# Moving two weight blocks ahead of the second half of the first x array, and four float32 second stages in place of six

## The chip, the cores and the metric

The kernel runs on one core of a Trainium2 chip. The metric is the device time of one execution in microseconds, as the median of several runs. Engines are named as in the profile: PE does matrix products (PEld is its weight load), DVE is the vector engine, ACT the scalar engine, POOL the GpSimd engine, and SP issues most of the DMA transfers. All inputs lie in HBM as the reference's types, so the two weight matrices and x are read in the layouts the host prepared, and the kernel does all the arithmetic.

## What is computed

The input x has 4 batches of 3008 rows of 256 numbers. A two-dimensional Fourier transform is taken of each batch and only its real part is kept; each of the 12032 rows then goes through a two-layer network with a SiLU between the layers.

```python
def _attn_ref(x):
    X = np.fft.fft(x, axis=1)
    X = np.fft.fft(X, axis=2)
    return X.real.astype(np.float32)

def _moe_ref(x, w_in, w_out):          # w_in 256 x 2048, w_out 2048 x 256
    h = x @ w_in
    g = h * (1.0 / (1.0 + np.exp(-h)))
    return (g @ w_out).astype(np.float32)
```

## The kernel before

The transform along the 256 columns is folded into w_in: `project(q)` multiplies a block of 256 of the 2048 columns of w_in with a cosine and sine table on PE, so there are eight blocks, q = 0 to 7. The transform along the rows is done by folding x (sums and differences on DVE and POOL) and multiplying the folded rows with cosine tables on PE. The result is cut into classes of columns that are laid one behind the other in chunks; the first chunk, c = 0, has 376 columns.

For each chunk c there are 16 steps f, one for each 128 of the 2048 hidden units. A step has these parts:

- `first(c, f)`: six matmuls on PE into a PSUM tile `pq`. There are two such tiles, so the first product of step n waits until DVE has read that of step n-2.
- `act(c, f)`: three DVE instructions (L420, L421, L422) make `h` from `pq`, then ACT applies SiLU. In chunk 0, for f < `FULL`, the result stays float32 (`g`, L427). Otherwise ACT writes SiLU (L433) and a rounded high part `gh` (L434), and DVE makes the rest `gl = h - gh` (`rest`, L446).
- `second(c, f)`: it runs three steps later (`LAG = 3`). With a float32 `g` it is one float32 matmul for each of four outputs (L461); otherwise it is three matmuls in the rounded type for each output (L463, L464, L470).

Step numbers n count from chunk 0, so in chunk 0 n = f. The weights arrive as 8-byte numbers. `load_w(q)` loads a block of w_in into a `win` tile (four of them), `upper(q)` on ACT (L78) and `lower(q)` on DVE (L82) put the float32 together, `convert(q)` is both, `project(q)` is its matmul (L533), `large(q)` on ACT (L538, L540) takes the high part `abh` out of PSUM, and `small(q)` on DVE (L544) makes the low part `abl`. `load_wo(q)`, `upper_wo`, `lower_wo` do the same for the eight blocks of w_out. A block of w_out with q < FULL/2 is kept in float32 (`wo_f32`) and split later by `split_wo` (L124 on ACT, L126 on DVE); the others are split at once by `high_wo` on ACT (L116) and `low_wo` on POOL (L119).

Before step 0 the start has to deliver the folded x rows of the first class. They come in three parts: `x2_first` (`first_x2`), and the two halves h = 0 and 1 of x1 (`load_first(h)`, one transfer of 512 KB called `raw` and two of 256 KB called `minus`; `first_x1` adds them up on DVE, L199 to L208). `product(a, i)` multiplies each part with its table (L597), `spread_first` moves the result from PSUM to the tile `uv` (ACT L394, DVE L396) and writes its first row `row0` (ACT L398). In step 0 `first_row` broadcasts this row with a matmul (L670) and an ACT copy (L671) into `ub`, which the first L420 needs.

The order of instructions is written out by hand and each engine runs its own in that order. The loads on SP's queue use eight semaphores in turn, so that each waits until the one eight places ahead of it has landed, and for its tile to be free. Between the steps two queues of deferred work are drained: one of DVE and ACT pieces that build the operand of the next class and run `split_wo`, and one of POOL pieces.

Of the kernel before, what the change touches and what calls it, by code (L numbers as in the profile page):

```python
# [42 lines left out]
STARTS = [sum(CHUNKS[:j]) for j in range(len(CHUNKS))]  # L43
LAST = len(CHUNKS) - 1
LAG = 3
FULL = 6
NF = DFF // 128


# [1 line left out]
def fft_mlp(ctx, tc, x1, x2, x2_first, w_in, w_out, te, to, t2, t2f, rot1, rot2, dft, out):  # L51
# [21 lines left out]
    def load_raw(t, block):  # L73
        nc.sync.dma_start(out=t[:, 1:1 + 8 * D].rearrange("p (c n) -> p c n", c=2), in_=block)  # L74

    def upper(dst, raw):
        flat = dst.rearrange("p c n -> p (c n)")
        nc.scalar.activation(flat.bitcast(F16)[:, 1::2], raw.bitcast(BF16)[:, 4:4 + 8 * D:4], AF.Copy)  # L78

    def lower(dst, raw):  # L80
        t = dst.rearrange("p c n -> p (c n)").bitcast(U32)
        stt(t, raw.bitcast(U32)[:, 1:1 + 4 * D:2], 13, t, op0=ALU.logical_shift_right, op1=ALU.bitwise_or)  # L82

    wo = [[wts.tile([128, 2, D], F32R, name=f"woh{f}") for f in range(NF // 2)], {}]
    wo_f32 = [wts.tile([128, 2, D], F32, tag="wof", name="wof", bufs=FULL // 2 + 1) for _ in range(FULL // 2)]
    for q in range(FULL // 2, NF // 2):
        wo[1][q] = wts.tile([128, 2, D], F32R, name=f"wol{q}")
# [6 lines left out]
    def load_wo(q):  # L94
        if 3 <= q < 6:
            t = wr.tile([128, RAW], U16, tag="win", name="wo", bufs=4)
        else:
            tag = {0: "ri0", 1: "xh", 2: "xl", 6: "ri0", 7: "ri1"}[q]
            t = (xs if tag[0] == "x" else fold_p).tile([128, RAW], U16, tag=tag, name="wo")
        wo_raw[q] = t  # L100
        load_raw(t, w_out[q * 256:(q + 1) * 256, :].bitcast(U16).rearrange("(f p) d -> p f d", p=128))
# [5 lines left out]
    def upper_wo(q):  # L107
        if q < FULL // 2:
            wo_wide[q] = wo_f32[q]
        upper(wo_wide[q], wo_raw[q])  # L110
# [10 lines left out]
    def split_wo(q):  # L121
        wf, wh = wo_f32[q], wo[0][q]
        wl = wo[1][q] = wts.tile([128, 2, D], F32R, tag="wof", name="wol", bufs=FULL // 2 + 1)
        nc.scalar.activation(wh, wf, AF.Copy)  # L124
# [265 lines left out]
    def spread_first(po):  # L390
        uvh, uvl, ub, n, _ = chunk(0)
        for i in range(2):
            p = po[i][:, 0, :n]
            nc.scalar.activation(uvh[:, i, :n], p, AF.Copy)  # L394
            yield
            tt(uvl[:, i, :n], p, uvh[:, i, :n].bitcast(F32), op=ALU.subtract)  # L396
            yield
        nc.scalar.activation(row0, p[0:1], AF.Copy)  # L398
        yield
# [3 lines left out]
    def first(c, f):  # L403
        uvh, uvl, _, n, _ = chunks[c]
        fs = slice(f * 128, (f + 1) * 128)
        pq = pqs[c, f] = pq_tile()
        for i in range(2):
            po = pq[:, i, :n]
            nc.tensor.matmul(po, abh[:, i, fs], uvh[:, i, :n], start=True, stop=False)  # L409
            nc.tensor.matmul(po, abh[:, i, fs], uvl[:, i, :n], start=False, stop=False)  # L410
            nc.tensor.matmul(po, abl[:, i, fs], uvh[:, i, :n], start=False, stop=True)  # L411
# [4 lines left out]
    def act(c, f, fill=()):  # L416
# [6 lines left out]
        for fn, q in fill:  # L423
            fn(q)
        if c == 0 and f < FULL:
            g = gp.tile([128, 2, CH], F32, tag=("gh", "gl")[f % 2], name="g")
# [12 lines left out]
    def rest(c, f):  # L439
        if c == 0 and f < FULL or (c, f) in rested:  # L440
            return
        rested.add((c, f))
        gh, gl, g = gs[c, f]
        n = chunks[c][3]
        for sg in signs(c, f):
            tt(gl[:, sg, :n], g[:, sg, :n], gh[:, sg, :n].bitcast(F32), op=ALU.subtract)  # L446
# [67 lines left out]
    win, wf32, pws = {}, {}, {}  # L514

    def load_w(q):
        win[q] = wr.tile([128, RAW], U16, tag="win", name="win", bufs=4)
        load_raw(win[q], w_in[:, q * 256:(q + 1) * 256].bitcast(U16).rearrange("(c p) f -> p c f", p=128))

    def clear(q):  # L520
        wf32[q] = fold_p.tile([128, 2, 256], F32, tag="half", name="wf", bufs=3)
        nc.gpsimd.memset(wf32[q], 0.0)

    def convert(q):
        upper(wf32[q], win[q])
        lower(wf32[q], win.pop(q))

    def project(q):
        w = wf32.pop(q)
        pw = pws[q] = ps.tile([128, 2, 256], F32, tag="ps", name="pw")  # L530
        for m in range(2):
            for c in range(2):
                nc.tensor.matmul(pw[:, m, :256], dft_sb[:, c, m, :], w[:, c], start=c == 0, stop=c == 1)  # L533

    def large(q):
        fs = slice(q * 256, (q + 1) * 256)
        row = rows[32 * (q % 4):32 * (q % 4) + 1, q // 4]
        nc.scalar.activation(row, pws[q][0:1, 1, :256].rearrange("o (f p) -> o p f", p=128), AF.Copy)  # L538
        nc.gpsimd.dma_start(out=a128[q], in_=row)
        nc.scalar.activation(abh[:, :, fs], pws[q][:, :, :256], AF.Copy)  # L540

    def small(q):
        fs = slice(q * 256, (q + 1) * 256)
        tt(abl[:, :, fs], pws.pop(q)[:, :, :256], abh[:, :, fs].bitcast(F32), op=ALU.subtract)  # L544
        for a in (abh, abl):
            nc.gpsimd.memset(a[0:1, 1, fs].bitcast(F32), 0.0)
# [10 lines left out]
    def load_first(h):  # L557
        t = raw_x[0, 0, h] = raws.tile([128, 4, D], F32, tag="raw", name="raw")
        nc.sync.dma_start(out=t, in_=x1[0, :, 0, h])
        for j in range(2):  # L560
            t = minus[h, j] = gp.tile([128, 2, D], F32, tag=("gh", "gl")[j], name="minus", bufs=LAG)
            nc.sync.dma_start(out=t, in_=x1[0, :, 1, h, 2 * j:2 * j + 2])
# [33 lines left out]
    def product(a, i):  # L596
        nc.tensor.matmul(po[i][:, 0, :CLASS[0][1]], x3[:, a, 128 * i:128 * i + 128], t2f_sb[:, a],  # L597
                         start=a == 2, stop=a == 1 - i)
# [1 line left out]
    convert(0)  # L600
    project(0)
    load_w(4)
    load_first(1)
    convert(1)
    project(1)
    clear(3)
    convert(2)
    large(0)
    project(2)
    clear(4)  # L610
    small(0)
    convert(3)
    load_w(5)
    load_w(6)
    load_w(7)
    for q in range(3):
        load_wo(q)
# [17 lines left out]
    lower(wf32[4], win.pop(4))  # L635
    load_wo(3)
    project(4)
    next(x1_work[1])
    large(3)
    next(x1_work[1])  # L640
    product(1, 0)
    product(1, 1)
    product(0, 1)
    upper(wf32[5], win[5])
    upper(wf32[6], win[6])
    small(1)
    lower(wf32[5], win.pop(5))
    load_wo(4)
    project(5)
    first_spread = spread_first(po)  # L650
    next(first_spread)
    next(first_spread)
    small(2)
    next(first_spread)
    next(first_spread)
    next(first_spread)
    lower(wf32[6], win.pop(6))
    load_wo(5)
    clear(7)
    small(3)  # L660
    large(4)
    upper(wf32[7], win[7])
    small(4)
    lower(wf32[7], win.pop(7))


    def first_row():
        n = CLASS[0][1]
        p = ps.tile([128, 512], F32, tag="ps", name="ub")[:, :n]
        nc.tensor.matmul(p, ones, row0, start=True, stop=True)  # L670
        nc.scalar.activation(chunk(0)[2][:, :n], p, AF.Copy)  # L671
# [63 lines left out]
    for n in range(len(steps) + LAG):  # L735
        c, f = steps[min(n, len(steps) - 1)]
        if n < len(steps):
            first(c, f)
        if n == 0:
            first_row()  # L740
            large(5)
        if n < 2:
            project(6 + n)
            large(6 + n)
        if n >= LAG:
            second(*steps[n - LAG])
        new = None
        if n < len(steps):
            turn = turns.get((c, f)) if n < len(steps) else None
            if turn:  # L750
                drain(queue, upto=("op", turn))
                drain(pool_queue, upto=("x", turn))
                new = pq_tile()
                transform(turn, new)
            act(c, f, fills.get(n, ()))
        if n == 0:
            small(5)
        if n == 1:
            small(6)
            small(7)  # L760
        for fn, q in after.get(n, ()):
            fn(q)
        if n == 2:
            late.close()
            acc_p = ctx.enter_context(tc.tile_pool(name="acc", bufs=1, space=PSUM))
            load_wo(7)
        if 1 <= n <= len(steps):
            rest(*steps[n - 1])
        if new:
            rest(c, f)  # L770
            spread(turn, new)
        if n < len(steps):
            for fn, a in plan.get((c, f), ()):
                fn(*a)
            drain(queue, 0.6)

            if f != 1 or c == 0 or pool_queue and pool_queue[0][0][0] == "x":
                drain(pool_queue, 1.3)
# [106 lines left out]
```

## Time and profile before

| what | us |
|---|---|
| median of 3 runs | 877.68 (877.65 to 877.82) |
| the profiled execution, whole time | 877.21 |
| its span on the core | 875.4 |
| PE busy in the span | 866.1 |
| DVE busy in the span | 706.2 |
| ACT busy in the span | 508.9 |
| POOL busy in the span | 197.9 |

The profile is of one execution, which was 0.47 us below the median. Starts are counted from the start of the span. Busy times of PE are modelled from pipelined matmuls; an engine's time shown as idle is followed by what released it. Consecutive instructions of one engine overlap a little, so the distance from one start to the next can be shorter than the duration in the row.

### The profile page before, as it was taken

What the parts mean: (1) busy time and instruction counts of PE and PEld (TensorE: products, weight loads), DVE (VectorE), ACT (ScalarE), POOL (GpSimd) and SP (SyncE); (2) the same over time, 40 slices, a digit from 0 to 9 for tenths busy, and PEclk for the clock granted to TensorE, in tenths of its full rate; (3) what the DMA queues carried; (4) which work ended last, traced back from release to release, by engine and by line L of the source; (5) the groups of instructions that cost most, each with busy time, mean ns of one, the idle gap of its engine ahead of it and who ended that gap; (6) DMA issues with size and microseconds to landing.
All of it is one profiled execution on the core that took longest, in us unless ns stands there. A gap on an engine that the chain in (4) does not pass through costs nothing.

```text
span 875.4 us, 11058 instructions
## 1 busy us (share of the span) xinstructions
PE 866.1 (99%) x4138; PEld 750.2 (86%) x4138; DVE 706.2 (81%) x994; ACT 508.9 (58%) x646; POOL 197.9 (23%) x243
## 2 busy tenths in 40 slices
PE   7999999999999999999999999999999999999998
PEld 6789999999998888888888888888888888888886
DVE  5999888888897887879778877888877877777774
ACT  4677756565765564557566455557546555455554
POOL 3475541312522220243312310050300110000000
PEclk9999999999999999999999999999999999999999
DMA  9955342236231433224225201323011021200101
GB/s 333 313 177 84 106 53 53 37 58 93 10 106 26 76 77 58 44 11 112 34 30 124 9 1 50 56 48 57 1 8 49 0 10 48 10 0 5 44 1 47
DMA packets 23413, 53.81 MB, mean 61 GB/s; under 512 B 3648, under 2 KB 12224, under 8 KB 22976
## 3 DMA queue, kind: packets, MB, share of 16 engines
q1 hardware_dynamic: 19632, 38.62, 20.4%
q0 software_dynamic: 3728, 14.49, 8.6%
q8 instruction: 32, 0.52, 0.3%
q14 instruction: 21, 0.17, 0.1%
HBM read 37.86 MB, written 12.34 MB: 57 GB/s over the span
## 4 chain that ended last, share of the span: by engine, by line
PE 97%; DMA 1%; DVE 1%; SPq 1%; issue 0%; ACT 0%; DVEq 0%
PE acc L470 20%; PE acc L464 20%; PE acc L463 20%; PE pq L409 10%; PE pq L410 10%; PE pq L411 10%; PE pq L340 5%; PE acc L461 2%; DMA minus<-in_x_dram 1%; PE pw L533 1%; PE pq L597 0%; SPq L74 0%; SPq L569 0%; DVE sm L204 0%; DVE sm L200 0%
## 5 line engine op out<-in xcount | busy, mean ns | idle before, releaser
L433 ACT ACTIVATE h<-h 128x1004 f32<-128x1004 f32 (+3 forms) x204 | 199.3, 977 | 303.6 <-DVE h L422 300.4
L463 PE MATMUL acc<-gh,woh 128*128 128x502 f32 (+2 forms) x808 | 302.2, 374 | 0.0
L464 PE MATMUL acc<-gh,wol 128*128 128x502 f32 (+2 forms) x808 | 302.2, 374 | 0.0
L446 DVE TENSOR_TENSOR gl<-h,gh 128x1004 fp32r<-128x1004 f32 (+3 forms) x204 | 237.9, 1167 | 14.7 <-ACT gh L434 14.0
L420 DVE SCALAR_TENSOR_TENSOR h<-ub,a,pq 128x502 f32<-128x502 f32 (+2 forms) x208 | 144.8, 696 | 96.7 <-PE pq L411 92.5
L470 PE MATMUL acc<-gl,woh 128*128 128x502 f32 (+2 forms) x808 | 210.3, 374 | 0.0
L434 ACT ACTIVATE gh<-h 128x1004 fp32r<-128x1004 f32 (+3 forms) x204 | 199.4, 977 | 6.5
L464 PEld LDWEIGHTS acc<-gh,wol 128*128 128x128 f32 x808 | 152.4, 189 | 22.4
L463 PEld LDWEIGHTS acc<-gh,woh 128*128 128x128 f32 x808 | 152.0, 188 | 22.3
L470 PEld LDWEIGHTS acc<-gl,woh 128*128 128x128 f32 x808 | 149.6, 188 | 23.2
L409 PE MATMUL pq<-uv,abh 128*128 128x502 f32 (+2 forms) x416 | 157.7, 379 | 0.0
L410 PE MATMUL pq<-uv,abh 128*128 128x502 f32 (+2 forms) x416 | 154.8, 372 | 0.0
L411 PE MATMUL pq<-uv,abl 128*128 128x502 f32 (+2 forms) x416 | 154.6, 372 | 0.0
L421 DVE TENSOR_TENSOR h<-h,pq 128x502 f32<-128x502 f32 (+2 forms) x208 | 132.7, 638 | 7.2
L422 DVE TENSOR_TENSOR h<-h,pq 128x502 f32<-128x502 f32 (+2 forms) x208 | 132.6, 638 | 7.2
L322 POOL TENSOR_TENSOR xl<-xf,xh 128x256 fp32r<-128x256 f32 x53 | 53.0, 1027 | 365.4 <-ACT xh L315 306.1
L409 PEld LDWEIGHTS pq<-uv,abh 128*128 128x128 f32 x416 | 78.1, 188 | 12.3 <-DVE h L422 0.5
L410 PEld LDWEIGHTS pq<-uv,abh 128*128 128x128 f32 x416 | 78.2, 188 | 11.7
L411 PEld LDWEIGHTS pq<-uv,abl 128*128 128x128 f32 x416 | 78.1, 188 | 11.4
L234 POOL TENSOR_TENSOR ri<-ri,raw 128x256 f32<-128x256 f32 x24 | 23.1, 978 | 57.6 <-ACT ri L229 57.3
L478 ACT ACTIVATE o<-acc 128x502 f32<-128x502 f32 (+2 forms) x52 | 27.9, 559 | 9.8 <-PE acc L470 7.7
L387 DVE TENSOR_TENSOR uv<-pq,uv 128x752 fp32r<-128x752 f32 (+4 forms) x21 | 14.5, 716 | 21.2 <-ACT row L383 21.1
(113 smaller groups left out, 472.5 us busy)
## 6 DMA issues: line engine op xcount, KB each, us to landing
raw<-in_x_dram SPq DMA_DIRECT2D x22, 512.0 KB, 6.3
raw<-in_x_dram POOLq DMA_DIRECT2D x20, 512.0 KB, 7.5
out_dram<-o SPq DMA_DIRECT2D x36, 251.0 KB, 2.2
win<-in_w_in_dram SPq DMA_DIRECT2D x8, 512.0 KB, 8.1
wo<-in_w_out_dram SPq DMA_DIRECT2D x8, 512.0 KB, 8.0
out_dram<-o SPq DMA_DIRECT2D x12, 188.0 KB, 2.3
ub<-row SPq DMA_DIRECT2D x8, 188.0 KB, 8.6
te<-in_te_dram POOLq DMA_DIRECT2D x1, 1128.0 KB, 5.5
```

The source lines that it names most:

```text
L409: nc.tensor.matmul(po, abh[:, i, fs], uvh[:, i, :n], start=True, stop=False)
L410: nc.tensor.matmul(po, abh[:, i, fs], uvl[:, i, :n], start=False, stop=False)
L411: nc.tensor.matmul(po, abl[:, i, fs], uvh[:, i, :n], start=False, stop=True)
L420: stt(p[:, :n], ub[:, :n], a128[f // 2][:, f % 2:f % 2 + 1], pq[:, 0, :n], op0=ALU.mult, op1=ALU.add)
L421: tt(h[:, 0, :n], p[:, :n], pq[:, 1, :n], op=ALU.add)
L422: tt(h[:, 1, :n], p[:, :n], pq[:, 1, :n], op=ALU.subtract)
L433: nc.scalar.activation(h[:, sg, :n], h[:, sg, :n], AF.Silu)
L434: nc.scalar.activation(gh[:, sg, :n], h[:, sg, :n], AF.Copy)
L446: tt(gl[:, sg, :n], g[:, sg, :n], gh[:, sg, :n].bitcast(F32), op=ALU.subtract)
L463: nc.tensor.matmul(po, wo[0][f // 2][:, f % 2, es], gh[:, sg, :n], start=f == 0, stop=False)
L464: nc.tensor.matmul(po, wo[1][f // 2][:, f % 2, es], gh[:, sg, :n], start=False, stop=False)
L470: nc.tensor.matmul(accs[c][i][:, :n], wo[0][f // 2][:, f % 2, es], gl[:, sg, :n], start=False, stop=f == NF - 1)
```

## The change

`FULL` goes from 6 to 4: steps 4 and 5 of chunk 0 and block 2 of w_out go the way of the later ones. In the start, the loads of w_in blocks 5 and 6 stand ahead of `load_first(1)` in SP's queue, and their conversion and projection stand ahead of `first_x1` of the second half. `small(1)` and `small(2)` move with them. Block 7 is converted before step 0 as it was, but projected within step 0, ahead of the first product of step 1, and not in step 1. `large` and `small` follow their blocks. Nothing is taken away from the start: all eight blocks are still loaded, converted and projected once.

```diff
--- before.py
+++ after.py
@@ -43,7 +43,7 @@
 STARTS = [sum(CHUNKS[:j]) for j in range(len(CHUNKS))]
 LAST = len(CHUNKS) - 1
 LAG = 3
-FULL = 6
+FULL = 4
 NF = DFF // 128
 
 
@@ -600,18 +600,18 @@
     convert(0)
     project(0)
     load_w(4)
-    load_first(1)
     convert(1)
     project(1)
+    load_w(5)
     clear(3)
     convert(2)
     large(0)
     project(2)
+    load_w(6)
+    load_first(1)
     clear(4)
     small(0)
     convert(3)
-    load_w(5)
-    load_w(6)
     load_w(7)
     for q in range(3):
         load_wo(q)
@@ -635,33 +635,34 @@
     lower(wf32[4], win.pop(4))
     load_wo(3)
     project(4)
+    small(1)
+    large(3)
+    convert(5)
+    load_wo(4)
+    project(5)
+    clear(7)
+    small(2)
+    convert(6)
+    load_wo(5)
+    project(6)
+    large(4)
     next(x1_work[1])
-    large(3)
+    large(5)
     next(x1_work[1])
     product(1, 0)
     product(1, 1)
     product(0, 1)
-    upper(wf32[5], win[5])
-    upper(wf32[6], win[6])
-    small(1)
-    lower(wf32[5], win.pop(5))
-    load_wo(4)
-    project(5)
+    small(3)
     first_spread = spread_first(po)
     next(first_spread)
     next(first_spread)
-    small(2)
+    small(4)
     next(first_spread)
     next(first_spread)
     next(first_spread)
-    lower(wf32[6], win.pop(6))
-    load_wo(5)
-    clear(7)
-    small(3)
-    large(4)
-    upper(wf32[7], win[7])
-    small(4)
-    lower(wf32[7], win.pop(7))
+    convert(7)
+    large(6)
+    small(5)
 
 
     def first_row():
@@ -738,10 +739,9 @@
             first(c, f)
         if n == 0:
             first_row()
-            large(5)
-        if n < 2:
-            project(6 + n)
-            large(6 + n)
+            project(7)
+        if n == 1:
+            large(7)
         if n >= LAG:
             second(*steps[n - LAG])
         new = None
@@ -754,9 +754,8 @@
                 transform(turn, new)
             act(c, f, fills.get(n, ()))
         if n == 0:
-            small(5)
+            small(6)
         if n == 1:
-            small(6)
             small(7)
         for fn, q in after.get(n, ()):
             fn(q)
```

Three places show how the instructions moved. The first is DVE around the second half of x1. L82 is `lower`, L544 is `small`, and L200 and L202 belong to `first_x1` of that half. This is one piece of the difference, with + for the changed kernel.

```order
 L208 TENSOR_TENSOR xf<-xf 128x127
 L82 SCALAR_TENSOR_TENSOR wf<-win,wf 128x512
+L544 TENSOR_TENSOR abl<-pw,abh 128x2x256
+L82 SCALAR_TENSOR_TENSOR wf<-win,wf 128x512
+L544 TENSOR_TENSOR abl<-pw,abh 128x2x256
+L82 SCALAR_TENSOR_TENSOR wf<-win,wf 128x512
 L200 TENSOR_TENSOR sm<-raw 128x512
 L202 TENSOR_TENSOR sm<-sm,minus 128x512
```

`small(1)`, `lower(5)`, `small(2)` and `lower(6)` now stand between `lower(4)` and the second half of x1; before, they followed it.

The second place is ACT from the two copies of the spread (L394) to the copy of the broadcast row into `ub` (L671, which is L672 in the changed kernel). Before:

```order
L394 ACTIVATE uv<-pq 128x376 x2
L398 ACTIVATE once<-pq 1x376
L538 ACTIVATE once<-pw 1x256
L540 ACTIVATE abh<-pw 128x2x256
L78 ACTIVATE wf<-win 128x512
L671 ACTIVATE ub<-ub 128x376
```

And in the changed kernel:

```order
L394 ACTIVATE uv<-pq 128x376 x2
L398 ACTIVATE once<-pq 1x376
L78 ACTIVATE wf<-win 128x512
L538 ACTIVATE once<-pw 1x256
L540 ACTIVATE abh<-pw 128x2x256
L672 ACTIVATE ub<-ub 128x376
```

The conversion of block 7 (L78) now stands ahead of a `large` (L538, L540, now that of block 6), and both still stand ahead of `ub`.

The third place is DVE in steps 5 and 6, where L82 is `lower_wo` and L300 to L301 are pieces of the next operand.

```order
 L422 TENSOR_TENSOR h<-h,pq 128x376
 L82 SCALAR_TENSOR_TENSOR wf<-wo,wf 128x512
+L446 TENSOR_TENSOR gl<-h,gh 128x2x376
 L300 TENSOR_TENSOR xf<-sm 64x129
 L301 TENSOR_TENSOR xf<-sm 64x127
```

An L446 is added there, and a second one in the same way a step later; they are the `gl` of steps 4 and 5.

## Rows read from the trace of the kernel before

**Rows 1.** The page: busy times of the engines; a costly group (busy, mean ns, idle).

```profile
PE 866.1 (99%) x4138; PEld 750.2 (86%) x4138; DVE 706.2 (81%) x994; ACT 508.9 (58%) x646; POOL 197.9 (23%) x243
...
L434 ACT ACTIVATE gh<-h 128x1004 fp32r<-128x1004 f32 (+3 forms) x204 | 199.4, 977 | 6.5
```

**Rows 2.** Busy time of each engine by stretch, then granted clock, DMA share, GB/s.

```profile
37.00:42.00 5.00, 5.00 (x21) 3.35 (x20) 4.90 (x11) 2.56 (x4) 3.36 (x8) 1.00 0.95 229
...
57.00:62.00 5.00, 5.00 (x30) 5.00 (x30) 4.83 (x6) 2.15 (x3) 5.00 (x6) 1.00 0.93 371
...
200.00:400.00 200.00, 199.99 (x973) 175.28 (x973) 165.56 (x236) 116.19 (x149) 50.47 (x57) 1.00 0.34 58
```

**Rows 3.** Waits of PE from 23 us to the end: us in total, times, longest.

```profile
PE pq L597 <- DVE xf L207: 0.9, 1, 0.9
```

**Rows 4.** Timeline of PE's weight load at step 13.

```profile
72.40 0.19 PEld L409 LDWEIGHTS pq<-uv,abh 128*128 128x128 f32 x1 [0.31 <-DVE uv L387]
```

**Rows 5.** Timeline of DVE in the start and step 0.

```profile
20.09 0.68 DVE L82 SCALAR_TENSOR_TENSOR wf<-win,wf 128x512 uint32<-128x512 uint32 x1
20.69 0.69 DVE L200 TENSOR_TENSOR sm<-raw 128x512 f32<-128x512 f32 x1
...
26.69 0.54 DVE L396 TENSOR_TENSOR uv<-pq,uv 128x376 fp32r<-128x376 f32 x1
...
30.02 0.60 DVE L420 SCALAR_TENSOR_TENSOR h<-ub,a,pq 128x376 f32<-128x376 f32 x1
...
31.70 0.68 DVE L544 TENSOR_TENSOR abl<-pw,abh 128x512 fp32r<-128x512 f32 x1
```

**Rows 6.** Timeline of ACT in the start.

```profile
19.09 0.78 ACT L78 ACTIVATE wf<-win 128x512 f16<-128x512 bf16 x1 [1.44 <-DMA win<-in_w_in_dram]
...
20.34 0.60 ACT L540 ACTIVATE abh<-pw 128x512 fp32r<-128x512 f32 x1
...
24.48 0.78 ACT L78 ACTIVATE wf<-win 128x512 f16<-128x512 bf16 x1 [0.29 <-DMA win<-in_w_in_dram]
...
25.93 0.48 ACT L394 ACTIVATE uv<-pq 128x376 fp32r<-128x376 f32 x1 [0.33 <-PE pq L597]
27.26 0.47 ACT L398 ACTIVATE once<-pq 1x376 f32<-1x376 f32 x1 [0.85 <-DVE uv L396]
...
...
30.01 0.37 ACT L538 ACTIVATE once<-pw 1x256 f32<-1x256 f32 x1
```

**Rows 7.** Timeline of SP's queue: issues of the third w_out block and of `rot_sb`.

```profile
20.28 0.37 SPq L74 DMA_DIRECT2D wo<-in_w_out_dram  x1
...
21.63 0.34 SPq L619 DMA_DIRECT2D rot_sb<-in_rot_dram  x1
```

**Rows 8.** The chain that ended last, in order of time: start, us, what.

```profile
23.75 2.13 PE pq L597 x6
...
28.64 0.82 PE ub L670 x2
...
32.42 1.73 PE pw L533 x8
...
36.19 2.69 PE acc L461 x8
...
39.91 2.53 PE acc L461 x8
...
57.67 0.17 PE acc L463
```

**Rows 9.** Timeline of DVE in steps 6 to 12.

```profile
53.16 0.94 DVE L446 TENSOR_TENSOR gl<-h,gh 128x752 fp32r<-128x752 f32 x1
...
57.79 1.48 DVE L446 TENSOR_TENSOR gl<-h,gh 128x752 fp32r<-128x752 f32 x1
...
71.40 0.95 DVE L387 TENSOR_TENSOR uv<-pq,uv 128x756 fp32r<-128x756 f32 x1
```

**Rows 10.** Timeline of POOL beside DVE's steps 7 and 8.

```profile
56.04 1.28 POOL L119 TENSOR_TENSOR wol<-wf,woh 128x512 fp32r<-128x512 f32 x1
```

## Prediction

> **What bounds the kernel now.** I read the page's busy times first: PE is busy for 866.1 of the span's 875.4 us [rows 1], so nearly all of the span is PE's own work, and a change to the start can win only PE's gaps and PE's work. The waits come next. From 23 us on, PE's matmuls wait once for longer than 0.3 us, 0.94 us for the second half of x1 [rows 3]. After that they run without a gap, which makes PE look like the only bound. The table by stretch tells more. DVE is busy 4.90 of 5 us around 40 us and 4.83 of 5 us from 57 to 62 us, but only 165.6 of 200 us later on [rows 2]. So from the start to step 13 DVE has no air either. The place to look at is where the two meet. The first product of step 13 starts at 72.40 us, after 0.31 us of waiting for DVE's L387 [rows 4], which started at 71.40 and took 0.95 us [rows 9]. L387 needs all that DVE has in its list before it, back to the first L420 at 30.02 us [rows 5]. **Whatever makes DVE's list from 30 to 72 us start later or grow longer therefore moves the first product of step 13, and nothing behind it gives it back**, since PE has no gaps there. Before I believe that a matmul saved in steps 4 and 5 is time saved, I have to add up DVE's list.
>
> **Step 1: the second half of x1 moves back.** What lands when: block 4 of w_in lands when ACT's L78 starts, at about 19.05 us, and block 6 at about 24.45 [rows 6]. Between them lie the 512 KB of `raw`, two `minus` of 256 KB, and blocks 5 and 6, four times 512 KB in 5.4 us, 1.35 us each. The wait for `raw`'s landing ended at 20.28 and that for the second `minus` at 21.63 [rows 7]. The same bytes in the new order land block 5 at 20.4, block 6 at 21.75, `raw` at 23.1, the two `minus` at 23.8 and 24.45 (estimates).
>
> DVE is the later one. `lower(4)` starts at 20.09 and the next instruction at 20.69 [rows 5], so one such instruction takes 0.60 us from start to start; L544 has the same size and gets the same price. In the changed kernel `small(1)` runs from 20.69 to 21.29. `lower(5)` needs ACT's `upper(5)`, which stands behind the L540 that starts at 20.34 and takes 0.60, and itself takes 0.78 [rows 6]: it ends at 21.72. Then `lower(5)`, `small(2)` and `lower(6)` take 3 x 0.60, and L200 starts at 23.52, where it started at 20.69: 2.83 us later. `upper(6)` is done by 22.6 and does not delay that. The transfers don't either: L200 needs `raw` (23.1), and the two adds 0.72 and 1.45 us later need 23.8 and 24.45. So the last three products start at 23.75 [rows 8] + 2.83 = 26.58 us. PE does blocks 5 and 6 meanwhile, 2 x 1.73 us [rows 8]: block 4 starts when its `lower` ends, at 20.8, and ends at 22.55, and block 6 ends at 26.0; its wait of 0.94 us shrinks to 0.6.
>
> **Step 2: from the products to the first L420.** Before, that took 30.02 - 23.75 = 6.27 us. Now the chain is this. The second L394 starts 2.18 us after the products' start (25.93) and takes 0.48; L396 takes 0.54 more and ends 3.25 us after the start, where it ended at 27.23, 3.48 after it. ACT then has L398, L78, L538, L540 and L671 in this order. Their durations are 0.47, 0.78, 0.37 and 0.60, and 0.48 for L671 as for L394, a copy of the same 376 columns [rows 6], less about 0.1 us of overlap for each but the last two: 0.38 + 0.65 + 0.39 + 0.60 + 0.48 = 2.5. With two hand-overs of 0.04 us, L420 starts 5.8 us after the products, at 32.4. DVE's own list gives the same: `upper(7)` ends 4.44 us after the products, `lower(7)` and `small(5)` follow, and that ends at 5.75. PE's broadcast (0.82 us, [rows 8]) is done before ACT gets to it. So **L420 starts 32.4 - 30.02 = 2.4 us later**. The projection of block 7 now stands ahead of the first product of step 1, 1.73 us that put this product at 33.5 to 34.5 us; DVE has the first h and `small(6)` until 34.75, so that wait costs nothing more.
>
> **Step 3: DVE's list from there to L387.** Out goes `small(5)`, which is now done before L420: 0.68 us [rows 5]. In come the two L446 of steps 4 and 5. Alone, one takes 0.94 us [rows 9], with the hand-over some 0.95 to 1.0 from start to start: +1.9. The third block of w_out is split on POOL, so one L126 also leaves DVE, but it stood behind step 13 and DVE has air there: nothing. ACT gets L433, L434 and L116 where one L427 stood, so DVE's next `lower_wo` and the operand piece behind it wait a little for ACT: I take 0.3 us, the least sure of these terms. Its ends are 0, if ACT is ahead of DVE there, and 1.0, one whole added L434 at its mean of 977 ns [rows 1], which is of larger tiles. Sum: -0.7 + 1.9 + 0.3 = **1.5 us longer**. The first product of step 13 starts 2.4 + 1.5 = 3.9 us later, at 76.3 us.
>
> **What PE saves, and why it doesn't count.** A float32 second stage takes 2.53 us (the one at 39.91), the other kind 12 x 0.17 = 2.07 [rows 8]. Two of them save 0.9 us of PE's work. PE then waits longer for DVE: with its own delays alone (below) step 13 would be ready some 3 us before DVE is.
>
> **Edits at nothing.** The loads of w_out behind the moved ones keep their places in SP's queue. On POOL, the split of block 2 now stands ahead of the two transfers that add to x1's next array and ahead of the tables' transfers; the tables are used by the products of the next class only, four steps behind, and both sides move by some 3 us. If that cover were gone, the wait would be the 1.3 us of one L119 [rows 10].
>
> **The sum.** The profiled execution took 877.21 us. With 3.9 more it is 881.1. It was 0.47 us below the median of 877.68, so the forecast on the median's footing is **881.6 us**.
>
> Bounds: without ACT's 0.3 us, and with L446 and the ACT chain 0.3 us cheaper each, +2.9: 880.6. With 1.0 us for ACT and the dearer L446 below, +5.7: 883.4.
>
> **Rivals.** *DVE and POOL collide.* The L446 at 57.79 took 1.48 us, in a stretch in which POOL was busy all the time [rows 2, 9]; the one at 53.16 took 0.94. In the changed kernel the two new L446 fall beside the splits of blocks 2 to 4 on POOL. If both take 1.48 us, the list is 2 x 0.54 = 1.1 us longer still: 882.7 us. The Trainium skill, page "SBUF — State Buffer", section "Who interferes with whom", states it as a lock: a DVE instruction with two SBUF inputs and a GpSimd instruction that reads SBUF block each other for a whole instruction. By that rule each new L446 could wait for a full L119; the 0.54 us that the trace shows are some 40% of an L119, and the measured duration is used.
>
> *DVE gives way and PE's own sum decides.* For: the page shows PE at 99%, and DVE's idle time in other stages shows that its list can be short. Against: the wait at step 13. Then only PE's delays count: the first product of step 3 waits for DVE's h of step 1, which ends at 36.6 (34.75, where DVE is done with `small(6)`, and three instructions), and the first second stage starts 1.03 us (six products) and a hand-over later, at 37.7, 1.5 us later than 36.19 [rows 8]; the two shorter stages give 0.9 back: +0.6, 878.3 us. That is not slower by what can be told. It decides if DVE's list from 30 to 72 us has more than 3.3 us of air, for instance if the six L446 of steps 6 to 11, of which that of step 7 took 0.54 us more than that of step 6, all run at the shorter duration because POOL's work now lies elsewhere.
>
> *Faster.* The second half of x1 is ready no later than PE's blocks 5 and 6, so that the 0.94 us gap [rows 3] closes, and the 0.9 us of matmuls are won as well: 877.68 - 1.84 = 875.8 us. Against it stand DVE's four instructions ahead of L200 and the 1 MB ahead of the second half in SP's queue; both would have to be wrong.
>
> **How the numbers follow.** About 0.2%, 1.75 us, is what can be told from no change. The forecast as worked out: 0.62. The collision: 0.20, slower too. PE's sum: 0.12, within 0.2%. Faster: 0.06. So slower 0.82, same 0.12, faster 0.06. The range takes in the bounds of the sum, the collision with ACT's upper end, and PE's sum: 878.2 to 884.0 us.
>
> **What the profile of the changed kernel would show.** L200 of the second half near 23.5 us and the products near 26.6 (step 1); the first L420 near 32.4 (step 2); DVE without gaps from there; the first product of step 13 near 76.3 us with PE waiting for DVE in several of the steps 3 to 13, some 3 us in all (step 3); and PE's distance from step 13 to the end as before. The prediction is wrong if the second half of x1 is added up before 22 us, if PE waits for DVE only at step 3, or if the L446 of steps 4 and 5 run in time that DVE had free.

## The result, and the profile of the changed kernel

| | us |
|---|---|
| before, median of 6 runs | 877.19 (876.38 to 877.82) |
| changed, median of 6 runs | 882.72 (882.61 to 884.74) |
| ratio, with its 95% interval | 1.0069 (1.0056 to 1.0082) |
| profiled execution of the changed kernel, whole time and span | 882.61, 880.8 |

The change makes the kernel slower by 0.6 to 0.8%: 5.5 us between the two medians, 4.9 to 7.2 us by the interval of the ratio; 3.9 us had been forecast. The page's row of busy times, to be set beside [rows 1], hardly moves: PE has 1.4 us more to do by the profile, and the span is 5.4 us longer.

```profile
PE 867.5 (98%) x4146; PEld 751.2 (85%) x4146; DVE 711.0 (81%) x995; ACT 510.8 (58%) x648; POOL 200.5 (23%) x244
```

The loss is in PE's waits from 22 us on (total us, times, longest), where [rows 3] had a single one:

```profile
PE pq L409 <- DVE h L422: 3.8, 5, 1.0
PE pq L409 <- DVE uv L387: 1.3, 1, 1.3
PE pw L533 <- DVE wf L82: 0.5, 1, 0.5
PE pq L597 <- DVE xf L207: 0.2, 1, 0.2
```

PE waits five times for DVE's `h` in steps 3 to 12 and once for L387 at step 13, 5.1 us in all. The table by stretch (busy time of PE, PEld, DVE, ACT, POOL with their counts; granted clock; DMA share; GB/s) has the same news: where [rows 2] show PE full, it now has holes, and DVE is as full as it was (47.5 of the 50 us from 30 to 80 us, in both traces).

```profile
57.00:62.00 5.00, 4.62 (x27) 4.22 (x26) 4.77 (x8) 3.86 (x5) 4.60 (x6) 1.00 0.99 392
62.00:69.00 7.00, 6.08 (x35) 5.46 (x34) 6.67 (x10) 4.42 (x8) 6.92 (x7) 1.00 0.52 205
69.00:75.00 6.00, 5.30 (x42) 5.14 (x41) 5.26 (x7) 3.83 (x6) 5.92 (x7) 1.00 0.00 0
75.00:80.00 5.00, 3.67 (x21) 3.36 (x21) 4.90 (x6) 3.70 (x10) 2.80 (x4) 1.00 0.47 17
```

To compare two traces a common zero is needed, since the first transfers of x take some 0.8 us more or less from one execution to the next. I take the start of DVE's first L199, which no change here moves. In the trace of before it is this row:

```profile
17.04 0.69 DVE L199 TENSOR_TENSOR raw<-raw,minus 128x512 f32<-128x512 f32 x1 [0.73 <-DMA minus<-in_x_dram]
```

The timeline of DVE in the changed kernel, at the four points of the forecast (the second L200 belongs to x1's second half):

```profile
16.20 0.69 DVE L199 TENSOR_TENSOR raw<-raw,minus 128x512 f32<-128x512 f32 x1 [0.71 <-DMA minus<-in_x_dram]
...
22.60 0.68 DVE L200 TENSOR_TENSOR sm<-raw 128x512 f32<-128x512 f32 x1
...
31.51 0.61 DVE L420 SCALAR_TENSOR_TENSOR h<-ub,a,pq 128x376 f32<-128x376 f32 x1
...
77.03 0.93 DVE L387 TENSOR_TENSOR uv<-pq,uv 128x756 fp32r<-128x756 f32 x1
```

And the timeline of PE at the three products of x1's second half and at step 13:

```profile
25.67 2.13 PE L597 MATMUL pq<-t2f,xf 128*128 128x376 f32 x6 [0.23 <-DVE xf L207]
...
78.02 0.45 PE L409 MATMUL pq<-uv,abh 128*128 128x376 f32 x1 [1.32 <-DVE uv L387]
```

| us after L199 | before [rows 4, 5, 8, 9] | changed | later by | forecast |
|---|---|---|---|---|
| L200 of the second half | 3.65 | 6.40 | 2.75 | 2.83 |
| its products | 6.71 | 9.47 | 2.76 | 2.83 |
| first L420 | 12.98 | 15.31 | 2.33 | 2.4 |
| first product of step 13 | 55.36 | 61.82 | 6.46 | 3.9 |
| end of the span | 858.36 | 864.60 | 6.24 | 3.9 |

Up to the first L420 the forecast holds within 0.1 us. From step 13 to the end nothing changes (803.0 and 802.8 us). The missing 2.6 us lie between these two points, in DVE's list. From the start of L420 to the end of L387 it took 42.33 us before and takes 46.45 us now, 4.1 us more where 1.5 were forecast. The next three fences show where: DVE's and then POOL's timeline of the changed kernel.

```profile
48.10 1.80 DVE L82 SCALAR_TENSOR_TENSOR wf<-wo,wf 128x512 uint32<-128x512 uint32 x1 [0.28 <-ACT wf L78]
49.83 0.93 DVE L446 TENSOR_TENSOR gl<-h,gh 128x752 fp32r<-128x752 f32 x1
...
51.27 1.30 DVE L297 TENSOR_TENSOR xf<-sm 128x129 f32<-128x129 f32 x1
...
54.97 0.93 DVE L446 TENSOR_TENSOR gl<-h,gh 128x752 fp32r<-128x752 f32 x1
...
58.11 1.37 DVE L446 TENSOR_TENSOR gl<-h,gh 128x752 fp32r<-128x752 f32 x1
...
61.25 1.34 DVE L82 SCALAR_TENSOR_TENSOR wf<-wo,wf 128x512 uint32<-128x512 uint32 x1
...
75.03 2.08 DVE L446 TENSOR_TENSOR gl<-h,gh 128x752 fp32r<-128x752 f32 x1 [0.71 <-ACT gh L434]
```

```profile
48.09 1.26 POOL L119 TENSOR_TENSOR wol<-wf,woh 128x512 fp32r<-128x512 f32 x1
51.07 1.34 POOL L119 TENSOR_TENSOR wol<-wf,woh 128x512 fp32r<-128x512 f32 x1 [1.72 <-ACT woh L116]
...
75.02 1.29 POOL L119 TENSOR_TENSOR wol<-wf,woh 128x512 fp32r<-128x512 f32 x1
```

The same instructions of DVE in the kernel before:

```profile
46.87 0.79 DVE L82 SCALAR_TENSOR_TENSOR wf<-wo,wf 128x512 uint32<-128x512 uint32 x1
...
48.17 0.30 DVE L297 TENSOR_TENSOR xf<-sm 128x129 f32<-128x129 f32 x1
...
56.06 1.80 DVE L82 SCALAR_TENSOR_TENSOR wf<-wo,wf 128x512 uint32<-128x512 uint32 x1
...
70.35 0.94 DVE L446 TENSOR_TENSOR gl<-h,gh 128x752 fp32r<-128x752 f32 x1 [0.69 <-PE pq L411]
```

A piece of the next operand, L297, takes 0.30 us alone and 1.30 us when POOL's L119 has started 0.20 us ahead of it; an L82 goes from 0.79 to 1.80 us with an L119 ahead by 0.01 us; the last L446 before L387 goes from 0.94 to 2.08. The two L446 that the change adds run undisturbed, at 0.93 us each. Worked out from start to start of these instructions:

| DVE's list, L420 to L387 | forecast | measured |
|---|---|---|
| `small(5)` out | -0.7 | -0.6 |
| two L446 in | +1.9 | +1.7 |
| wait for ACT ahead of L82 | +0.3 | +0.4 |
| L82 at 48.10 beside L119 | 0 | +1.0 |
| L297 at 51.27 beside L119 | 0 | +1.0 |
| L446 of step 6, 0.94 [rows 9] to 1.37 | 0 | +0.4 |
| L82 of block 6, 1.80 to 1.34, and a wait ahead of it | 0 | -0.7 |
| last L446, beside L119 | 0 | +1.0 |
| sum (4.1 by the list's two ends) | 1.5 | 4.2 |

The first three terms come to 1.5 us measured, as forecast. All the rest, 2.7 us net, are instructions of DVE that POOL works beside: both L82, L297 and the last L446 stand beside or just behind an L119, and the L446 of step 6 stands behind POOL's L322, which starts at 57.95 us. The list is not quite without gaps, in either kernel: DVE waits 0.7 us for ACT's `gh` ahead of the last L446, so the L446 before that one has some air.

The last row of the table needs care, since the profiled execution of before had a tie there that came out well for DVE. This is POOL's row of before:

```profile
70.37 2.09 POOL L119 TENSOR_TENSOR wol<-wf,woh 128x512 fp32r<-128x512 f32 x1
```

DVE's last L446 started at 70.35, and POOL was the one that took longer. The experiments come back to whether most executions of before fare like this.

### The profile page after: what moved, and what is told of

Same layout as the page of the kernel before. It is cut to its first block, busy times and chain, and to the rows that moved or that the text cites. A ratio compares the mean times of both kernels' runs of the same rounds, so it can differ in the third digit from the quotient of the medians.

```text
span 880.8 us, 11079 instructions
## 1 busy us (share of the span) xinstructions
PE 867.5 (98%) x4146; PEld 751.2 (85%) x4146; DVE 711.0 (81%) x995; ACT 510.8 (58%) x648; POOL 200.5 (23%) x244
## 4 chain that ended last, share of the span: by engine, by line
PE 91%; DVE 1%; issue 0%; ACT 0%; DVEq 0%
PE acc L470 19%; PE acc L463 19%; PE acc L464 19%; PE pq L409 10%; PE pq L410 9%; PE pq L411 9%; PE pq L340 5%; DVE h L420 0%; DVE gl L446 0%; DVE h L421 0%; DVE uv L387 0%; ACT gh L434 0%; ACT h L433 0%; DVE wf L82 0%; DVE h L422 0%
## 5 line engine op out<-in xcount | busy, mean ns | idle before, releaser
L446 DVE TENSOR_TENSOR gl<-h,gh 128x1004 fp32r<-128x1004 f32 (+3 forms) x206 | 242.3, 1177 | 15.1 <-ACT gh L434 15.1
L420 DVE SCALAR_TENSOR_TENSOR h<-ub,a,pq 128x502 f32<-128x502 f32 (+2 forms) x208 | 144.8, 696 | 96.2 <-PE pq L411 92.0
L421 DVE TENSOR_TENSOR h<-h,pq 128x502 f32<-128x502 f32 (+2 forms) x208 | 132.7, 638 | 7.2
L422 DVE TENSOR_TENSOR h<-h,pq 128x502 f32<-128x502 f32 (+2 forms) x208 | 132.6, 638 | 7.1
L322 POOL TENSOR_TENSOR xl<-xf,xh 128x256 fp32r<-128x256 f32 x53 | 53.5, 1037 | 362.8 <-ACT xh L315 319.4
L387 DVE TENSOR_TENSOR uv<-pq,uv 128x752 fp32r<-128x752 f32 (+4 forms) x21 | 14.5, 716 | 21.0 <-ACT row L383 21.0
```

Of the source, the lines that this page charges most:

```text
L420: stt(p[:, :n], ub[:, :n], a128[f // 2][:, f % 2:f % 2 + 1], pq[:, 0, :n], op0=ALU.mult, op1=ALU.add)
L421: tt(h[:, 0, :n], p[:, :n], pq[:, 1, :n], op=ALU.add)
L422: tt(h[:, 1, :n], p[:, :n], pq[:, 1, :n], op=ALU.subtract)
```

## The experiments

Theory: the time is set by DVE's list from the first L420 to L387, which starts later by the new order and grows by two L446 and by meetings with POOL's L119. Rivals: PE's own delays in steps 0 to 3 set the time (and DVE's list has air), or the added instructions cost PE directly.

**The parts alone: `FULL` and the order.** The kernel before with one number changed:

```diff
-FULL = 6
+FULL = 4
```

> The kernel before with FULL = 4 alone; the order of the start is as before. Theory A (DVE's list from the first L420 to L387 sets step 13): the first L420 stays near 30 us, the list grows by the two L446, 1.9 us, and the time by 1.6 to 1.9 us if nothing collides. Theory C (as A, and DVE's instructions with two SBUF inputs are stretched where POOL's L119 reads SBUF at the same time): one more L119 now falls into the list, so up to 2 us more, +2 to +4 us. Theory B (PE's own sum sets the time): two second stages of 2.07 us for two of 2.53, so -0.9 us.

Measured: 881.14 us against 877.36, ratio 1.0045 (1.0028 to 1.0062), +3.8 us. DVE's timeline has the three meetings of the changed kernel at the same instructions:

```profile
46.80 1.80 DVE L82 SCALAR_TENSOR_TENSOR wf<-wo,wf 128x512 uint32<-128x512 uint32 x1 [0.28 <-ACT wf L78]
...
49.97 1.30 DVE L297 TENSOR_TENSOR xf<-sm 128x129 f32<-128x129 f32 x1
...
73.75 2.10 DVE L446 TENSOR_TENSOR gl<-h,gh 128x752 fp32r<-128x752 f32 x1 [0.70 <-ACT gh L434]
```

So they are there without the new order: `FULL = 4` gives POOL one L119 more and shifts the others. (The first two are only there with `FULL = 4`; the last L446 also took 2.10 us in the next kernel, where `FULL` is 6, so that one does not need `FULL = 4`.) The float32 stages that it saves on PE don't show in the time at all.

The other part is the changed kernel with `FULL` put back:

```diff
-FULL = 4
+FULL = 6
```

> The changed kernel with FULL = 6, so only the order of the start is changed. Theory A: the first L420 comes 2.4 us later than before and one L544 (0.7 us) leaves the list, step 13 and the time +1.7 us. Theory C adds nothing of its own, since no L119 is added: +1.7 us, give or take 0.5 for other overlaps. Theory B: the first second stage comes 1.0 to 1.5 us later and nothing is given back: +1.0 to +1.5 us. With e1 the two parts should add up to the whole change, 5.5 us, under A and C.

Measured: 880.83 us (879.09 to 881.73), ratio 1.0038 (1.0025 to 1.0051), +3.5 us. Two of the five executions, with a mean granted clock of 0.999 to 1.000, took 879.09 and 879.90 us, 2.1 us over before; the forecast's own terms for the order alone are 2.4 - 0.7 = 1.7. The other three had a mean clock of 0.997. The profiled one is of those; its table by stretch (columns as above, the third number from the end is the granted clock) and PE's timeline show the place:

```profile
28.00:33.00 5.00, 4.39 (x13) 2.73 (x14) 3.50 (x7) 2.97 (x6) 1.64 (x5) 0.83 1.07 373
33.00:37.00 4.00, 3.79 (x16) 3.11 (x15) 2.21 (x4) 2.48 (x4) 1.09 (x3) 0.79 0.58 223
...
33.00:34.00 1.00, 1.00 (x4) 0.73 (x4) 1.00 (x2) 0.51 (x1) 0.00 (x0) 0.50 1.03 410
```

```profile
31.04 3.57 PE L533 MATMUL pw<-wf,once 128*128 128x256 f32 x8 [0.46 <-DVE wf L82]
```

PE had been busy with short gaps since 25.6 us, the last of them 0.46 us, while it waited for block 7; then the clock fell from 2.4 to 1.2 GHz for part of this stretch (0.50 from 33 to 34 us), and block 7's projection took 3.57 us. In the profiled execution of the changed kernel, at full clock, the same instruction group took 1.99 us.

**Is it that gap?** The kernel with the new order and `FULL = 6`, with one more float32 matmul in the gap, whose result is unused (the trace has it as two, 0.70 us together):

```diff
             first_row()
+            zeros(1)
             project(7)
```

> The changed order of the start with FULL = 6 (as e2_order), with one more matmul of zeros (about 0.43 us, its result unused) in PE's gap of 0.46 us ahead of block 7's projection. If the fall of the granted clock to 0.83 around 30 to 40 us comes from PE's gaps between 25.6 and 31 us: clock 1.00 in all runs and 1.9 to 2.5 us over before, where e2_order had 3.5 to 4.4 in three of five. If the fall has nothing to do with that gap: the same mixture of runs as e2_order.

Measured: 879.19 us against 877.73, ratio 1.0015 (1.0005 to 1.0024), +1.5 us, and all ten executions at a clock of 0.999 or 1.000.

```profile
28.00:33.00 5.00, 4.86 (x19) 2.84 (x18) 3.54 (x7) 2.97 (x6) 1.64 (x5) 1.00 1.07 371
33.00:37.00 4.00, 3.18 (x18) 2.81 (x17) 3.85 (x8) 2.95 (x5) 1.09 (x3) 1.00 0.60 231
```

Of the kernels in the new order without that matmul (the changed one, the one with `FULL = 6` above, and two below), 7 of 19 executions had a mean clock of 0.998 or less. That fits the gap as the cause, but the numbers are small, and these ten executions ran on another chip than the five with `FULL = 6`, so it is not shown. What is shown is that the new order has a second cost that the forecast did not know: some 1.5 to 2 us in some of the executions, by the clock. The median of the changed kernel is not one of these. The undisturbed order costs 1.5 to 2.1 us, `FULL = 4` 3.8, and together that is the whole of the loss, 5.5 to 6 us.

**Does DVE's list bind, or is it PE?** Before, with two spare instructions in the shape of L446 in steps 4 and 5, whose result nobody reads; PE's, ACT's and POOL's work is as before:

```diff
     def rest(c, f):
+        if c == 0 and f in (4, 5) and (c, f) not in rested:
+            rested.add((c, f))
+            if f == 4:
+                spare.append(xs.tile([128, 1280], F32, tag="xl", name="spare"))
+            g = gs[c, f][:, :, :376]
+            tt(spare[0][:, :752].rearrange("p (a n) -> p a n", a=2), g, g, op=ALU.subtract)
```

> The kernel before with two more DVE instructions of an L446's size, at the places where the changed kernel's added L446 stand; their results are not used. PE's work is that of before. Theory A: DVE's list is longer by 2 x 0.95 us, of which the 0.3 us that PE waited at step 13 is not air but already a wait: time +1.6 to +1.9 us. Theory B: DVE has air, time +0.0 to +0.4 us.

Measured: 880.05 us, ratio 1.0031 (1.0019 to 1.0042), +2.7 us. PE's waits from 22 us on:

```profile
PE pq L409 <- DVE h L422: 1.5, 2, 0.8
PE pq L409 <- DVE uv L387: 1.3, 1, 1.3
PE pq L603 <- DVE xf L207: 0.9, 1, 0.9
```

Nothing was added but time on DVE, and PE waits 2.8 us for `h` and L387, where it had waited 0.3 us. In the trace DVE's list is 3.4 us longer and step 13 comes 3.4 us later: the list had no air there. That ends the rival in which DVE gives way and PE's own sum decides. Here too the list grew by more than the two instructions, 3.4 us against 1.7, by meetings: an L301 of 0.28 us took 1.27, and the last L446 took 2.09.

**Are the meetings with L119 the missing term?** The changed kernel with POOL's L119 replaced by a fill that reads nothing; the low parts of w_out blocks 2 to 7 are left out of the result by it:

```diff
-        nc.gpsimd.tensor_tensor(wo[1][q], wo_wide.pop(q), wo[0][q].bitcast(F32), op=ALU.subtract)
+        wo_wide.pop(q)
+        nc.gpsimd.memset(wo[1][q].bitcast(F32), 0.0)
```

> The changed kernel with POOL's L119 replaced by a POOL memset of zeros of the same tile: it leaves out the low parts of the w_out blocks 2 to 7, and POOL no longer reads SBUF there. Theory C: the DVE rows of the changed kernel that stood beside an L119 and took 1.80, 1.30 and 2.08 us (L82 at 48.1, L297 at 51.3, L446 at 75.0) go back to 0.7, 0.3 and 0.9 us; the time falls by 2.5 to 3.5 us, to 2 to 3.5 us above the kernel before. Theory A without C: those rows are long for another reason and stay; the time changes by less than 0.5 us. Theory B: no change.

Measured: 880.89 us (879.46 to 881.54), ratio to before 1.0040 (1.0025 to 1.0055). Two of the four executions had the lower clock; the other two took 879.46 and 880.27, 2.5 us over before, so that some 3 us of the changed kernel's loss are gone. All three instructions are back at the length that they have alone (DVE's timeline, in which L298 and L447 are L297 and L446 of the other kernels):

```profile
50.00 0.69 DVE L82 SCALAR_TENSOR_TENSOR wf<-wo,wf 128x512 uint32<-128x512 uint32 x1 [0.28 <-ACT wf L78]
...
52.05 0.29 DVE L298 TENSOR_TENSOR xf<-sm 128x129 f32<-128x129 f32 x1
...
74.91 0.94 DVE L447 TENSOR_TENSOR gl<-h,gh 128x752 fp32r<-128x752 f32 x1 [0.92 <-ACT gh L435]
```

The profiled execution is one with the lower clock, and its list of 45.11 us holds a wait of 1.67 us for PE's slow matmuls that the changed kernel (46.45 us) does not have:

```profile
35.82 0.61 DVE L421 SCALAR_TENSOR_TENSOR h<-ub,a,pq 128x376 f32<-128x376 f32 x1 [1.67 <-PE pq L412]
```

Without that wait the list would be 3.0 us shorter than in the changed kernel, which agrees with the times.

The same edit in the kernel before:

> The kernel before, with POOL's L119 (the low part of w_out blocks 3 to 7) replaced by a fill with zeros that reads nothing; that low part is left out of the result. Theory (DVE's list from the first L420 to L387 sets the start of step 13 in the changed kernel, and in the kernel before it has only just enough room): DVE's list gets about 2 us shorter, the 0.3 us wait at step 13 goes, and PE bounds alone: 0 to 0.3 us faster than before, no more. Rival (L119 beside other work costs time as such, in any kernel): as in the changed kernel, where the same edit gave some 2 to 4 us, so 874 to 875.

Measured: 877.03 us, ratio 0.9991 (0.9982 to 1.0001), -0.7 us, which is not clear of nothing. There it is worth little, as the theory says: the meetings count only where PE waits for DVE's list.

**Shortening the list another way.** Two deferred splits and the conversion of w_out block 7 go behind step 13; first in the changed kernel:

```diff
-        at(*divmod(2 * q + 9, NF), add, queue, ("wo", q), split_wo(q))
+        at(*divmod(2 * q + 14, NF), add, queue, ("wo", q), split_wo(q))
...
-    for q, n in enumerate((0, 1, 2, 3, 4, 5, 7, 9)):
+    for q, n in enumerate((0, 1, 2, 3, 4, 5, 7, 12)):
```

> The changed kernel, with the two deferred splits of w_out blocks 0 and 1 five steps later and the conversion of w_out block 7 three steps later, so that they stand behind step 13 in DVE's list. Theory: one L126 (0.87 us) and one L82 (0.68 us) leave DVE's list before L387, and the last L446 before it no longer meets POOL's L119 (0.95 us): 2.5 us less in the list, all of it on the path: 2.0 to 2.5 us faster than the changed kernel, some 3.8 to 4.3 us slower than before. Rival (the time lies in PE's delays in steps 0 to 3 or in POOL's chain): no change against the changed kernel, 6.3 slower than before.

Measured: 881.99 us, ratio to before 1.0052 (1.0037 to 1.0067), +4.3 us where the changed kernel has 5.5. That is at the upper end of what was expected, and the list itself got shorter by only 1.0 us (45.45) and not by 2.5: the moved work brought two later L446 level with POOL's folds of x, or just behind their start. DVE, then POOL:

```profile
65.86 2.09 DVE L446 TENSOR_TENSOR gl<-h,gh 128x752 fp32r<-128x752 f32 x1
...
69.73 1.69 DVE L446 TENSOR_TENSOR gl<-h,gh 128x752 fp32r<-128x752 f32 x1
```

```profile
65.86 1.28 POOL L218 TENSOR_TENSOR raw<-raw 128x512 f32<-128x512 f32 x1
...
69.34 1.27 POOL L218 TENSOR_TENSOR raw<-raw 128x512 f32<-128x512 f32 x1
```

The same edit in the kernel before (where it moves three splits), twice, and the kernel before as a kernel of its own beside the second:

> The same edit in the kernel before. Theory: the same 2 us or so leave DVE's list, but PE waits there for only 0.3 us: 0 to 0.3 us faster than before. Rival (these pieces cost their time wherever PE is): 2 us faster.

> The kernel before with the two deferred splits five steps later and w_out block 7 converted three steps later, a second time (the first gave 1.28 us less, where 0 to 0.3 was expected). If DVE's list is all there is to it: 0 to 0.5 us faster, and the first gap came from differences between runs. If these instructions cost time in PE too: 1.0 to 1.5 us faster again, and PE's records from step 13 on show where.

> The kernel before, unchanged, as a kernel of its own: how far apart two sets of executions of one program lie here, and its profile on the same chip as the three others. Expected: ratio 1.000 within 0.0005; a wait of PE of about 0.3 us at step 13.

Measured: 876.45 us, ratio 0.9985 (0.9976 to 0.9994), and 876.37 us, 0.9987 (0.9978 to 0.9995); the kernel before against itself 0.9999 (0.9990 to 1.0008). So this version is faster than both kernels, by 0.05 to 0.24%, and by more than the theory's 0.3 us. The traces don't show the 1.2 us: from L199 to the end the profiled execution of before took 858.35 us (858.36 in the first trace) and that of this version 858.17. What the traces do show is a tie. In both profiles of before the last L446 and POOL's L119 start within 0.02 us, and DVE is ahead; POOL's L119 then takes 2.1 us and DVE loses nothing. Had POOL been ahead, as in the changed kernel (75.02 and 75.03), step 13 would start about 1 us later. The records can't tell who will win: with `FULL = 6` in the new order DVE's start is 0.01 us ahead of POOL's 73.09, and DVE loses all the same.

```profile
73.08 2.10 DVE L446 TENSOR_TENSOR gl<-h,gh 128x752 fp32r<-128x752 f32 x1 [0.70 <-ACT gh L434]
```

In all five traces of other kernels that have this meeting DVE loses, and in both of before it wins. The 27 executions of before in that batch range over 2.3 us (876.38 to 878.69), the 11 of this version over 0.9 us. The ten kernels profiled at full clock in their first 800 us also show 0.6 to 1.3 us more against before in the traces, from L199 to the end, than in the medians. All this would follow if most executions of before lose that tie. A sum over the traces says the same: an execution's time is the start of its L199, what follows, and 1.8 us outside the span. L199 starts at 15.7 to 17.1 us in the fourteen traces, 16.4 in the middle. With 858.35 us behind it the median of before in this batch, 877.5, would need a start at 17.4, later than in any trace; with 1 us more it needs 16.4. But no profile of an execution of before that loses the tie was taken, so it stays argued. If it holds, the last row of the table above is no cost of the change in most executions, and the meetings cost it 1.7 us and not 2.7. That is what the medians say too: 5.5 us measured, less 3.9 forecast, is 1.6.

**Can the two L446 be made free?** `FULL = 4` alone, with the splits late as above and w_out blocks 6 and 7 converted at steps 11 and 12; and the same with `FULL = 6`:

```diff
-    for q, n in enumerate((0, 1, 2, 3, 4, 5, 7, 9)):
+    for q, n in enumerate((0, 1, 2, 3, 4, 5, 11, 12)):
```

> Only FULL = 4, in the start's order of before, with the splits of the float32 blocks five steps later and w_out blocks 6 and 7 converted at steps 11 and 12, behind step 13's first products in DVE's list. FULL = 4 alone gave 3.8 us more. Theory: out of DVE's list before L387 go one L126 (0.87 us), two L82 (0.7 and 1.3 us) and the meeting of the last L446 with L119 (1.1 us), 4.0 us in all, so that the list is within 1 us of that of before, and PE's saved 0.9 us begins to count: between 1.2 us faster than before (PE alone, if no other collision appears) and 1 us slower. Rival (the added L446, L433 and L434 cost PE time wherever DVE is): 3 to 4 us slower, as FULL = 4 alone.

> The same moves with FULL = 6, as in the kernel before. Theory: DVE's list gets shorter by 3 us and PE waits for it nowhere; what is left is PE's own time: 0.3 us faster than before, no more. If w_out block 6 is now ready too late for its second stage at step 15: slower, with a wait of PE for POOL's L119.

Measured: 880.67 us, ratio 1.0035 (1.0021 to 1.0048), and 878.60 us, 1.0011 (1.0002 to 1.0020). Both were expected lower. The first is at its rival's number, but not for the rival's reason: DVE's list is 44.25 us, 1.9 more than before, and in both kernels PE loses more than 1 us from 80 to 100 us, where before it lost none. The first kernel's row, then the second's:

```profile
80.00:100.00 20.00, 18.48 (x102) 16.94 (x101) 19.17 (x28) 14.55 (x23) 12.76 (x14) 1.00 0.59 143
80.00:100.00 20.00, 18.84 (x106) 17.58 (x105) 19.13 (x30) 14.87 (x22) 11.75 (x12) 1.00 0.52 119
```

The second kernel, without `FULL = 4`, has the cause in the timelines of ACT, DVE and PE:

```profile
73.78 0.51 ACT L229 ACTIVATE ri<-raw,rot_sb 128x256 f32<-128x256 f32 x1 [2.65 <-DVE wf L82]
```

```profile
77.92 1.21 DVE L82 SCALAR_TENSOR_TENSOR wf<-wo,wf 128x512 uint32<-128x512 uint32 x1 [2.50 <-ACT raw L226]
```

```profile
82.47 0.44 PE L409 MATMUL pq<-uv,abh 128*128 128x378 f32 x1 [0.72 <-DVE h L422]
```

Block 6 of w_out is loaded into the tile that L229 writes later. Converted so late, it holds up ACT for 2.65 us, and with it the conversion of block 7 that stands behind L229 on ACT, DVE behind that, and PE. The wait that my move took away came back with another name. Against its own partner `FULL = 4` still costs 2.1 us here, so these moves did not make it free.

## Why the prediction was right, and where its size was off

- **What bounds the kernel.** Right: the time is lost at step 13 and at the steps ahead of it, in PE's waits for DVE, while the page shows PE at 99% before and 98% after. Two spare instructions on DVE cost 2.7 us, with PE's work unchanged, so DVE's list bounds the time up to step 13, behind the PE that the page shows.
- **Step 1** (x1's second half moves back by 2.83 us): 2.75 us. Right, DVE's four instructions ahead of L200 and not the transfers set it. PE's gap ahead of the products shrank from 0.94 to 0.23 us, where 0.6 was forecast; it lies on no path that counts.
- **Step 2** (the first L420 2.4 us later): 2.33 us. Right by the chain over ACT. By itself the order cost 2.1 us at full clock and 1.5 us with PE's gap filled. Not foreseen: in some executions the clock falls behind PE's new waits up to 31 us.
- **Step 3** (DVE's list 1.5 us longer) is the term that was mis-sized: 4.1 us between the two profiled executions, and some 3.1 us if most executions of before lose their tie. Its three named parts came out as forecast. What was set at nothing is the list's meetings with POOL. The prediction had them as a rival, and priced them for the two new L446 alone, at 0.54 us each from the L446 of step 7 [rows 9]. These two met nothing: DVE ran them between the splits, not beside them. An L82, an L297 and the last L446 met an L119, at 1.0 us each. The row to price it by was there: in the trace of before the L82 at 56.06 us took 1.80 us, 0.02 us behind the L119 of [rows 10], and not 0.68 [rows 5].
- **"Edits at nothing", POOL.** The added split of block 2 was checked for POOL's own lateness (the tables, the transfers) and found free. It was not asked what DVE runs beside it, nor what the shift of the other splits does. This is where the 2.7 us come from.
- **What PE saves.** Right that the 0.9 us of two float32 stages don't count: `FULL = 4` alone is 3.8 us slower, and it still costs 2.1 us with DVE's list cut.
- **The rivals.** "DVE gives way and PE's own sum decides" falls with the two spare instructions. "Faster" falls with the result. "DVE and POOL collide" had the right cause at the wrong places, and that its 882.7 us is the measured 882.72 is luck: 1.1 us forecast for two instructions, 2.7 us measured for five, and the median of before, from which 882.7 was counted, came down by 0.5 us with three more runs.
- **The range.** It held the measured time by room that was set aside for other reasons, ACT's upper end and two dearer L446. ACT's wait came out near the forecast, at 0.4 us for 0.3.
- **Small slips.** 12 x 0.17 is 2.04 and not 2.07; no conclusion hangs on it.

DVE's wait behind POOL is described by the Trainium skill, page "SBUF — State Buffer", section "Who interferes with whom": a DVE instruction with two inputs in SBUF and a GpSimd instruction that reads SBUF block each other for the whole instruction, and whoever issues first goes on. The traces agree where the two start together (0.30 to 1.30, 0.94 to 2.08 us, beside an L119 of 1.3 us); the prediction set the rule's full wait aside for the 0.54 us of one row, and for these instructions the rule was nearer. L421 and L422, with one input in PSUM, kept their 0.55 us beside POOL throughout.

## What to carry to other kernels

Where a saturated engine is fed by a list on another engine that has no air, add up that list to the point where they meet; the saved work of the saturated engine counts for nothing until the list is short again. When an edit adds or shifts work on POOL, go through what DVE runs at that time, and price every DVE instruction with two SBUF inputs there with and without a whole POOL instruction ahead of it, the short ones too. A piece moved off the list must also be followed to the tile that it frees: here a conversion moved by four steps held up ACT's writes to the same tile.

## What the runs showed of the hardware that was not expected

- Which of DVE and POOL waits can come out either way when they start together. The last L446 and an L119 whose starts lie at most 0.02 us apart take 0.94 and 2.1 us in the two traces of before, and 2.08 and 1.29 us in the changed kernel. The loser's extra time is about the winner's length, and only the first case is free for this kernel.
- In kernels whose PE has gaps of 0.2 to 0.5 us between 25 and 31 us, 7 of 19 executions had a lower mean clock. In a profiled one the granted clock fell to half behind these gaps, and eight matmuls took 3.57 us in place of 1.99. With one more float32 matmul in the last gap, 10 of 10 executions kept the clock; that the gap is the cause is likely, not shown.
- One profiled execution need not be the typical one. From L199 on, the two traces of before agree to 0.01 us, and yet the other kernels differ from before by 0.6 to 1.3 us more in the traces than in the medians.
